# Moving mask making and small loads to GpSimd, and one more load ahead of the opening barrier, in a one-token decode block

## The chip, the cores and the metric

The kernel runs on one core of one Trainium2 chip. The metric is the device time of one execution in microseconds, measured over several executions. The profile is one of those executions, taken by the hardware profiler; its span is about 1.9 us shorter than the measured time. Times inside a profile count from the start of the span.

## The reference

One token (a row `x` of 576 numbers) goes through two branches that a gate mixes. Branch A is attention with 32 query heads over 16 key-value heads and the last 4096 positions of a cache, head size 128. Branch B is a dense layer with gelu, 576 to 4608 to 576.

```python
g = sigmoid((x * gate_w).sum(-1, keepdims=True))
# A: sliding-window attention on a cache
q = (x @ wq).reshape(B, Sq, 32, 128)
scores = einsum("bhqd,bhkd->bhqk", q, k[-4096:]) * 128**-0.5
a = einsum("bhqk,bhkd->bhqd", softmax(scores), v[-4096:]).reshape(...) @ wo
# B: dense gelu
b = gelu(x @ w1 + b1) @ w2 + b2
out = g * a + (1 - g) * b
```

All of `k`, `v`, `wq`, `wo`, `w1`, `w2` have to be read once: 53.6 MB in bf16. With one token there is little arithmetic for each byte.

## The kernel before

The large loads all go out on SyncE's queue, in the order w1, wq, k (eight halves of groups), w2 first half, v (four groups), wo, w2 second half. They share a few large buffers, tagged A to D, so a load can only be issued when the earlier tenant of its buffer has been used. The first part of w1 is moved ahead of the program's opening barrier by editing the instruction list.

```python
    def first_load_ahead(nc):
        main, body = nc.main_func.blocks[0], nc.main_func.blocks[1]
        first = next(i for i in body.instructions
                     if i.engine == mybir.EngineType.SP and type(i).__name__ == "InstDMACopy")
        body.instructions.remove(first)
        at = next(n for n, i in enumerate(main.instructions) if i.engine == mybir.EngineType.SP)
        main.instructions.insert(at, first)
    nc.at_finalize(first_load_ahead)
    # small loads, on ScalarE's queue
    nc.scalar.dma_start(out=x_row, in_=A_x.rearrange("a b d -> (a b) d"))
    nc.scalar.dma_start(out=gw_row, ...); nc.scalar.dma_start(out=b2_row, ...)
    nc.scalar.dma_start(out=b1_t, ...)
    # ... w1 (two parts) into tag "B", wq into tag "A", on nc.sync ...
```

VectorE makes the masks from an identity matrix, by reductions and sixteen small copies, and prepares `x2`, the column form of `x` that the first stage multiplies with w1 and wq:

```python
    par = ...; nc.vector.reduce_sum(out=par[:], in_=ident_f[:].rearrange("p (a t) -> p t a", t=2), axis=AX.X)
    for t in range(2):
        nc.vector.tensor_copy(out=alt[:, t : NI + 1 : 2], in_=par[:, t : t + 1].to_broadcast(...))
    # ... x doubled and turned by nine matmuls into xs_ps ...
    for t in range(2):
        nc.vector.tensor_tensor(out=x2[:, :, t], in0=xs_ps[:], in1=alt[:, t : t + NI], op=ALU.mult)
    # ... lo32, hi4, lo8, pen, pen2 by reductions ...
    for j in range(4):
        for b in range(4):
            nc.vector.tensor_copy(out=perm[:, j, b, :], in_=idv[:, j // 2, :, j % 2])
    # ... first stage: h_ps (162 matmuls on w1), gelu on VectorE, q_ps (144 matmuls on wq) ...
    for g in range(NG):
        k_t = big.tile([P, 2, SL, Dh], BF16, name="k_t", tag="CDBA"[g])   # waits for the buffer
        # ... per half: load, VectorE transposes (kt), 16 matmuls into s_ps
    nc.vector.reduce_max(out=m2[:], in_=s_ps[:].rearrange("p (n b) -> p b n", b=2), axis=AX.X)
    # ... softmax; w2 first half in tag "B"; v groups in tags "CDAC"; wo; w2 second half
```

## Time and profile before

The kernel before took 133.99 us. The table has what matters, each from the view named.

| Reading | Value | View |
|---|---|---|
| bytes moved, mean rate | 53.78 MB, 407 GB/s | page, DMA queues |
| rate while the queue is full | about 427 GB/s, DMA share about 1.0 | busy time by stretches |
| VectorE busy, GpSimd busy | 55.4 us, 0.7 us | page, engines |
| first stage (h_ps) | 12.80 to 23.02 us | timeline |
| last weights used from | 128.25 us | timeline |

First the page of the kernel before: the busy line, then busy time in forty slices of 3.3 us for the DMA engines, then the DMA queues and the chain of work that ended last.

```profile
PE 77.4 (59%) x1126; PEld 51.1 (39%) x1126; DVE 55.4 (42%) x80; ACT 12.9 (10%) x25; POOL 0.7 (1%) x6
DMA  7999998999999999999999999999999999999960
...
q8 instruction: 9, 0.15, 0.4%
q10 hardware_dynamic: 10, 0.01, 0.0%
q14 instruction: 1, 0.01, 0.0%
...
DMA 67%; PE 12%; DVE 8%; ACT 7%; issue 2%; SPq 1%; DVEq 0%
```

No engine is busy more than 59% of the span, but the DMA row reads 9 (90% or more), once 8, from the second slice nearly to the end. That points to a kernel bound by its bytes. The queue lines are packets, MB and share; the small q14 line will matter later.

Next the busy time of the engines by stretches, kernel before. The columns are the stretch, its length, busy time and count of PE, PEld, DVE, ACT and POOL, the granted clock, the DMA share and GB/s. The share can pass 1 slightly because packets are counted with the time they were under way.

```profile
4.00:20.00 16.00, 10.74 (x149) 9.60 (x150) 5.77 (x38) 0.17 (x1) 0.00 (x0) 1.00 1.04 446
20.00:60.00 40.00, 29.03 (x281) 15.74 (x281) 27.52 (x20) 1.45 (x6) 0.00 (x0) 1.00 0.99 420
60.00:100.00 40.00, 21.30 (x343) 13.52 (x341) 19.10 (x17) 9.66 (x16) 0.00 (x0) 0.75 1.00 429
100.00:126.00 26.00, 13.79 (x321) 10.76 (x322) 0.48 (x2) 0.00 (x0) 0.00 (x0) 0.59 1.00 420
```

The DMA share is 0.99 or more in all four stretches, whatever the engines do. Last, the front in the timeline of the kernel before (start, length, engine, line, operation, and in brackets the idle time before it with what ended it):

```profile
0.79 0.51 ACTq L83 DMA_DIRECT2D rows<-in_A_x_dram  x1
1.48 1.83 DVE L216 MEMSET qz_flat<- 128x2128 f32 x1 [0.39 <-issue]
6.29 0.85 DVE L117 COPY rows<-rows 1x576 bf16<-1x576 bf16 x2 [2.98 <-DMA rows<-in_A_x_dram]
11.61 0.23 DVE L130 TENSOR_TENSOR x<-xs_ps,alt 128x9 bf16<-128x9 f32 x2
23.06 0.20 DVE L228 COPY hacc<-h_ps 128x36 f32<-128x36 f32 x1 [9.39 <-PE h_ps L219]
```

The token's own 1,152 bytes were issued at 0.79 us and used at 6.29 us. w1's packets were then already under way, which is the likely reason. `x2` came at 11.6 us, behind other small VectorE work.

### The profile page before, as it was taken

What the parts mean: (1) busy time and instruction counts of PE and PEld (TensorE: products, weight loads), DVE (VectorE), ACT (ScalarE), POOL (GpSimd) and SP (SyncE); (2) the same over time, 40 slices, a digit from 0 to 9 for tenths busy, and PEclk for the clock granted to TensorE, in tenths of its full rate; (3) what the DMA queues carried; (4) which work ended last, traced back from release to release, by engine and by line L of the source; (5) the groups of instructions that cost most, each with busy time, mean ns of one, the idle gap of its engine ahead of it and who ended that gap; (6) DMA issues with size and microseconds to landing.
All of it is one profiled execution on the core that took longest, in us unless ns stands there. A gap on an engine that the chain in (4) does not pass through costs nothing.

```text
span 132.1 us, 2458 instructions
## 1 busy us (share of the span) xinstructions
PE 77.4 (59%) x1126; PEld 51.1 (39%) x1126; DVE 55.4 (42%) x80; ACT 12.9 (10%) x25; POOL 0.7 (1%) x6
## 2 busy tenths in 40 slices
PE   0038999084699769769779460007942952456651
PEld 0035999084234323223223230007942952333430
DVE  6059100503978988988985710653000000100001
ACT  3000000003000000000000059940000000000001
POOL 2000000000000000000000000000000000000000
PEclk9999999999999999999999996555555555556998
DMA  7999998999999999999999999999999999999960
GB/s 246 421 443 411 448 518 368 398 427 427 427 417 432 422 431 419 427 436 417 454 408 442 451 446 417 407 466 427 397 451 387 431 417 428 429 407 427 406 249 0
DMA packets 3190, 53.78 MB, mean 407 GB/s; under 512 B 358, under 2 KB 362, under 8 KB 620
## 3 DMA queue, kind: packets, MB, share of 16 engines
q1 hardware_dynamic: 3170, 53.61, 95.7%
q8 instruction: 9, 0.15, 0.4%
q10 hardware_dynamic: 10, 0.01, 0.0%
q14 instruction: 1, 0.01, 0.0%
HBM read 53.62 MB, written 0.00 MB: 406 GB/s over the span
## 4 chain that ended last, share of the span: by engine, by line
DMA 67%; PE 12%; DVE 8%; ACT 7%; issue 2%; SPq 1%; DVEq 0%
DMA k_t<-in_A_k_cache_dram 26%; DMA w_t<-in_B_w_dram 21%; DMA wq_t<-in_A_wq_dram 20%; ACT p_t L351 7%; PE o_ps L402 5%; DVE kt L300 3%; PE q_ps L257 3%; DVE pt L359 2%; DVE m L321 2%; PE s_ps L309 1%; PE y_ps L193 1%; SPq L415 1%; PE t_ps L377 0%; DVE out_row L437 0%; SPq L417 0%
## 5 line engine op out<-in xcount | busy, mean ns | idle before, releaser
L300 DVE STREAM_TRANSPOSE kt<-k_t 128x2048 f32<-128x2048 f32 x16 | 36.0, 2290 | 9.7 <-DMA k_t<-in_A_k_cache_dram 9.7
L309 PE MATMUL s_ps<-kt,qz_flat 128*128 128x512 bf16 x128 | 32.3, 399 | 9.2 <-DVE kt L300 9.2
L309 PEld LDWEIGHTS <-qz_flat 128*128 128x128 bf16 x128 | 12.8, 100 | 28.3 <-issue 14.7
L402 PE MATMUL o_ps<-pt,v_t 128*128 128x8 bf16 x512 | 14.6, 168 | 8.5 <-DMA v_t<-in_A_v_cache_dram 6.5
L402 PEld LDWEIGHTS <-v_t 128*128 128x128 bf16 x512 | 14.3, 104 | 8.9 <-DMA v_t<-in_A_v_cache_dram 6.7
L351 ACT ACTIVATE p_t<-s_ps,negm 128x512 bf16<-128x512 f32 x8 | 9.7, 1412 | 44.9 <-DVE negm L342 44.9
L219 PE MATMUL h_ps<-x,w_t 128*128 128x2 bf16 x162 | 10.2, 202 | 0.0
L219 PEld LDWEIGHTS <-w_t 128*128 128x128 bf16 x162 | 10.1, 169 | 0.0
L420 DVE TENSOR_TENSOR om<-o_ps,rgh 128x128 bf16<-128x128 f32 x1 | 0.3, 292 | 22.2 <-PE o_ps L402 22.2
L193 PE MATMUL y_ps<-wo_t,ov 128*1 128x288 bf16 x64 | 6.1, 364 | 4.6 <-DMA wo_t<-in_A_wo_dram 4.6
L359 DVE STREAM_TRANSPOSE pt<-p_t 128x2048 bf16<-128x2048 bf16 x2 | 4.6, 2312 | 7.4 <-ACT p_t L351 7.4
L377 PE MATMUL t_ps<-ls,ones 128*128 128x32 f32 x2 | 0.6, 396 | 11.9 <-DVE ls L375 11.9
L193 PE MATMUL y_ps<-w_t,gt 128*1 128x288 bf16 x72 | 5.6, 285 | 2.1 <-DMA w_t<-in_B_w_dram 2.1
L437 DVE CAST out_row<-y_ps 1x288 bf16<-1x288 f32 x1 | 0.4, 446 | 15.1 <-PE y_ps L193 15.1
L257 PE MATMUL q_ps<-x,wq_t 128*128 128x2 bf16 x144 | 4.0, 166 | 4.0 <-DMA wq_t<-in_A_wq_dram 4.0
L193 PEld LDWEIGHTS <-ov 128*1 128x1 bf16 x64 | 3.4, 103 | 7.0 <-issue 4.5
L257 PEld LDWEIGHTS <-wq_t 128*128 128x128 bf16 x144 | 3.9, 104 | 4.0 <-DMA wq_t<-in_A_wq_dram 4.0
L377 PEld LDWEIGHTS t_ps<-ls,ones 128*128 128x128 f32 x2 | 0.5, 310 | 12.2 <-issue 12.2
L120 PE MATMUL xs_ps<-one_b,rows 1*128 1x1 bf16 x9 | 0.7, 195 | 7.2 <-DVE rows L117 7.2
L193 PEld LDWEIGHTS <-gt 128*1 128x1 bf16 x72 | 3.2, 83 | 3.9 <-issue 2.9
L436 ACT CAST out_row<-y_ps 1x288 bf16<-1x288 f32 x1 | 0.4, 390 | 42.2 <-PE y_ps L193 42.2
L228 DVE COPY hacc<-h_ps 128x36 f32<-128x36 f32 x1 | 0.2, 196 | 9.4 <-PE h_ps L219 9.4
(68 smaller groups left out, 28.7 us busy)
## 6 DMA issues: line engine op xcount, KB each, us to landing
k_t<-in_A_k_cache_dram SPq DMA_DIRECT2D x8, 2048.0 KB, 32.3
v_t<-in_A_v_cache_dram SPq DMA_DIRECT2D x3, 4096.0 KB, 29.8
wq_t<-in_A_wq_dram SPq DMA_DIRECT2D x1, 4608.0 KB, 25.8
wo_t<-in_A_wo_dram SPq DMA_DIRECT2D x2, 2304.0 KB, 20.2
v_t<-in_A_v_cache_dram SPq DMA_DIRECT2D x2, 2048.0 KB
w_t<-in_B_w_dram SPq DMA_DIRECT2D x1, 2880.0 KB, 14.1
w_t<-in_B_w_dram SPq DMA_DIRECT2D x1, 2592.0 KB, 11.3
w_t<-in_B_w_dram SPq DMA_DIRECT2D x1, 2304.0 KB, 8.0
```

The lines of the kernel that those rows point to most:

```text
L120: nc.tensor.matmul(xs_ps[:, i : i + 1], lhsT=xdup[:, i : 2 * D : NI], rhs=one_b[0:1, 0:1], start=(i == 0), stop=(i == NI - 1), skip_group_ ...
L193: nc.tensor.matmul(y_out[s], lhsT=vec, rhs=row[:, s * DH : (s + 1) * DH], start=start, stop=stop, skip_group_check=True,)
L219: nc.tensor.matmul(h_ps[:, j:NF:NJ], lhsT=w1_t[:, i, j:FH:NJ], rhs=x2[:, i, :], start=False, stop=(i == NI - 1 and j == NJ - 1), skip_grou ...
L257: nc.tensor.matmul(q_ps[:, j : Hq : Hq // 2], lhsT=wq_t[:, i, j * Dh : (j + 1) * Dh], rhs=x2[:, i, :], start=(i == 0 and j == 0), stop=(i ...
L300: nc.vector.transpose(out=kt[:, u * half : (u + 1) * half].bitcast(FP32), in_=k_t[:, f, u * SL // 2 : (u + 1) * SL // 2, :] .rearrange("p ...
L309: nc.tensor.matmul(s_ps[:, u * 512 : (u + 1) * 512].rearrange("p (c k) -> p c k", k=32), lhsT=qz[:, h0 // 2, j, :], rhs=kv[:, u * SL // 4 ...
L321: nc.vector.reduce_max(out=m2[:], in_=s_ps[:].rearrange("p (n b) -> p b n", b=2), axis=AX.X)
L351: nc.scalar.activation(out=p_t[:, cs, :, b], in_=s_ps[:].rearrange("p (c k u b) -> p u b c k", k=8, u=2, b=2)[:, f, b % 2], func=ACT.Exp, ...
L359: nc.vector.transpose(out=pt[:, cs, :].rearrange("p c h -> p (c h)"), in_=p_t[:, cs, :, :].rearrange("p c k b -> p (c k b)"),)
L377: nc.tensor.matmul(t_ps[:], lhsT=ones[:], rhs=ls[:], start=True, stop=True)
L402: nc.tensor.matmul(o_ps[:, 8 * g : 8 * g + 8, 0], lhsT=v_t[:, c, :], rhs=pt[:, c, 8 * g : 8 * g + 8], start=(c == 0), stop=(c == NCK - 1),)
L415: nc.sync.dma_start(out=wo_t[:, r0:r1, :], in_=wo_src[:, r0:r1, :])
```

## The change

Its intent is to get the first stage going earlier: take the mask work off VectorE, make the masks with GpSimd's iota, compare and select, clear `qz_flat` there, move three small loads to GpSimd's queue, and issue x's load ahead of the opening barrier as w1's already is. The diff, cut to its core:

```diff
-    def first_load_ahead(nc):
+    def first_loads_ahead(nc):
+        for engine in (mybir.EngineType.SP, mybir.EngineType.Activation):
+            # ... the same move, for the first load of each of the two engines
-    nc.scalar.dma_start(out=gw_row, ...)   # and b2_row, b1_t
+    nc.gpsimd.dma_start(out=gw_row, ...)   # and b2_row, b1_t
-    nc.vector.memset(one_b[:], 1.0)
+    nc.gpsimd.memset(one_b[:], 1.0)
+    for base, pattern, keep in (...five masks...):
+        nc.gpsimd.iota(low[:, c0 : c0 + n], pattern=pattern, base=base, channel_multiplier=1)
+        nc.gpsimd.memset(mask[:, c0 : c0 + n], keep)
+    nc.vector.tensor_tensor(out=low[:], in0=low[:], in1=mask[:], op=ALU.bitwise_and)
+    nc.gpsimd.tensor_scalar(out=is0[:], in0=low[:], scalar1=0.0, scalar2=None, op0=ALU.is_equal)
+    nc.gpsimd.memset(perm[:], 0.0)
+    nc.gpsimd.affine_select(out=perm[:], in_=perm[:], pattern=[[-64, 2], [-1, 2], [0, 4], [-2, 32]], ...)
-    # par, alt, lo32, hi4, lo8, pen, pen2 by reductions; sixteen perm copies (all on VectorE)
-    for t in range(2):
-        nc.vector.tensor_tensor(out=x2[:, :, t], in0=xs_ps[:], in1=alt[:, t : t + NI], op=ALU.mult)
+    nc.vector.tensor_tensor(out=x2[:], in0=xs_ps[:].to_broadcast([P, NI, 2]), in1=alt, op=ALU.mult)
-    nc.vector.memset(qz_flat[:].bitcast(FP32), 0.0)
+    nc.gpsimd.memset(qz_flat[:].bitcast(FP32), 0.0)
-    # p1 = hacc * r_t, then gt = p1 * omg
+    # gt = hacc * omg * r_t in one scalar_tensor_tensor
```

More of the change, by code (lines that the diff above doesn't have):

```diff
@@ L10 @@
 BF16 = mybir.dt.bfloat16
+I32 = mybir.dt.int32
 ACT = mybir.ActivationFunctionType
@@ L51 @@
     SCALE = 1.0 / (Dh**0.5)
-    def first_load_ahead(nc):
+    def first_loads_ahead(nc):
         main, body = nc.main_func.blocks[0], nc.main_func.blocks[1]
-        first = next(
-            i
-            for i in body.instructions
-            if i.engine == mybir.EngineType.SP and type(i).__name__ == "InstDMACopy"
-        )
-        body.instructions.remove(first)
-        at = next(
-            n for n, i in enumerate(main.instructions) if i.engine == mybir.EngineType.SP
-        )
-        main.instructions.insert(at, first)
-    nc.at_finalize(first_load_ahead)
+        for engine in (mybir.EngineType.SP, mybir.EngineType.Activation):
+            first = next(
+                i
+                for i in body.instructions
+                if i.engine == engine and type(i).__name__ == "InstDMACopy"
+            )
+            body.instructions.remove(first)
+            at = next(n for n, i in enumerate(main.instructions) if i.engine == engine)
+            main.instructions.insert(at, first)
+    nc.at_finalize(first_loads_ahead)
     const = ctx.enter_context(tc.tile_pool(name="const", bufs=1))
@@ L83 @@
     nc.scalar.dma_start(out=x_row, in_=A_x.rearrange("a b d -> (a b) d"))
-    nc.scalar.dma_start(out=gw_row, in_=gate_w.rearrange("(o n) -> o n", o=1))
-    nc.scalar.dma_start(out=b2_row, in_=B_b2.rearrange("(o n) -> o n", o=1))
-    nc.scalar.dma_start(out=b1_t, in_=B_b1.rearrange("(h n) -> h n", h=2))
+    nc.gpsimd.dma_start(out=gw_row, in_=gate_w.rearrange("(o n) -> o n", o=1))
+    nc.gpsimd.dma_start(out=b2_row, in_=B_b2.rearrange("(o n) -> o n", o=1))
+    nc.gpsimd.dma_start(out=b1_t, in_=B_b1.rearrange("(h n) -> h n", h=2))
     w1_t = big.tile([P, NI, FH], BF16, name="w1_t", tag="B")
@@ L99 @@
     one_b = const.tile([1, 2], BF16, name="one_b")
-    nc.vector.memset(one_b[:], 1.0)
+    nc.gpsimd.memset(one_b[:], 1.0)
+    NCC = 2 * NI + 32 + 4 + 6
+    low = const.tile([P, NCC], I32, name="low")
+    mask = const.tile([P, NCC], I32, name="mask")
+    c0 = 0
+    for base, pattern, keep in (
+        (0, [[1, NI], [1, 2]], 1),
+        (128, [[-1, 32]], 31),
+        (128, [[-32, 4]], 96),
+        (8, [[-2, HB]], 6),
+        (4, [[-2, 2]], 2),
+    ):
+        n = 1
+        for step, num in pattern:
+            n *= num
+        nc.gpsimd.iota(low[:, c0 : c0 + n], pattern=pattern, base=base, channel_multiplier=1)
+        nc.gpsimd.memset(mask[:, c0 : c0 + n], keep)
+        c0 += n
@@ L101 @@
+    nc.vector.tensor_tensor(out=low[:], in0=low[:], in1=mask[:], op=ALU.bitwise_and)
+    is0 = const.tile([P, NCC], FP32, name="is0")
+    nc.gpsimd.tensor_scalar(
+        out=is0[:], in0=low[:], scalar1=0.0, scalar2=None, op0=ALU.is_equal
+    )
+    alt = is0[:, 0 : 2 * NI].rearrange("p (i t) -> p i t", t=2)
+    lo32 = is0[:, 2 * NI : 2 * NI + 32]
+    hi4 = is0[:, 2 * NI + 32 : 2 * NI + 36]
     ones = const.tile([P, P], FP32, name="ones")
-    nc.vector.memset(ones[:], 1.0)
+    nc.gpsimd.memset(ones[:], 1.0)
@@ L103 @@
     ident = const.tile([P, P], BF16, name="ident")
     make_identity(nc, ident[:])
-    ident_f = const.tile([P, P], FP32, name="ident_f")
-    nc.vector.tensor_copy(out=ident_f[:], in_=ident[:])
-    par = const.tile([P, 2], FP32, name="par")
-    nc.vector.reduce_sum(out=par[:], in_=ident_f[:].rearrange("p (a t) -> p t a", t=2), axis=AX.X)
-    alt = const.tile([P, NI + 1], FP32, name="alt")
-    for t in range(2):
-        nc.vector.tensor_copy(
-            out=alt[:, t : NI + 1 : 2], in_=par[:, t : t + 1].to_broadcast([P, (NI + 1) // 2])
-        )
@@ L116 @@
-    for t in range(2):
-        nc.vector.tensor_copy(out=xdup.rearrange("p (d t) -> p d t", t=2)[:, :, t], in_=x_row)
-    xs_ps = ps_m.tile([P, NI], FP32, name="xs_ps", tag="m")
+    perm = const.tile([P, 4, 4, 32], BF16, name="perm")
+    nc.gpsimd.memset(perm[:], 0.0)
+    nc.gpsimd.affine_select(
+        out=perm[:],
+        in_=perm[:],
+        pattern=[[-64, 2], [-1, 2], [0, 4], [-2, 32]],
+        compare_op=ALU.not_equal,
+        fill=1.0,
+        base=0,
+        channel_multiplier=1,
+    )
@@ new lines @@
+    ident_f = const.tile([P, P], FP32, name="ident_f")
+    nc.gpsimd.tensor_copy(out=ident_f[:], in_=ident[:])
+    lo32b = const.tile([P, 32], BF16, name="lo32b")
+    nc.gpsimd.tensor_copy(out=lo32b[:], in_=lo32)
+    pens = const.tile([P, HB + 2], FP32, name="pens")
+    nc.gpsimd.tensor_scalar(
+        out=pens[:],
+        in0=is0[:, 2 * NI + 36 : NCC],
+        scalar1=1e30,
+        scalar2=-1e30,
+        op0=ALU.mult,
+        op1=ALU.add,
+    )
+    pen = pens[:, 0:HB]
+    pen2 = pens[:, HB : HB + 2]
@@ L119 @@
+    nc.vector.tensor_copy(
+        out=xdup.rearrange("p (d t) -> p d t", t=2),
+        in_=x_row.rearrange("p (d o) -> p d o", o=1).to_broadcast([1, D, 2]),
+    )
+    xs_ps = ps_m.tile([P, NI, 1], FP32, name="xs_ps", tag="m")
     for i in range(NI):
         nc.tensor.matmul(
-            xs_ps[:, i : i + 1],
+            xs_ps[:, i, :],
             lhsT=xdup[:, i : 2 * D : NI],
@@ L128 @@
     x2 = const.tile([P, NI, 2], BF16, name="x2")
-    for t in range(2):
-        nc.vector.tensor_tensor(
-            out=x2[:, :, t], in0=xs_ps[:], in1=alt[:, t : t + NI], op=ALU.mult
-        )
-    lo32 = const.tile([P, 32], FP32, name="lo32")
-    nc.vector.reduce_sum(out=lo32[:], in_=ident_f[:].rearrange("p (a t) -> p t a", t=32), axis=AX.X)
-    lo32b = const.tile([P, 32], BF16, name="lo32b")
-    nc.vector.tensor_copy(out=lo32b[:], in_=lo32[:])
-    hi4 = const.tile([P, 4], FP32, name="hi4")
-    nc.vector.reduce_sum(out=hi4[:], in_=ident_f[:].rearrange("p (a t) -> p a t", t=32), axis=AX.X)
-    lo8 = const.tile([P, 8], FP32, name="lo8")
-    nc.vector.reduce_sum(out=lo8[:], in_=ident_f[:].rearrange("p (a c) -> p c a", c=8), axis=AX.X)
-    pen = const.tile([P, HB], FP32, name="pen")
-    nc.vector.reduce_sum(out=pen[:], in_=lo8[:].rearrange("p (b t) -> p b t", t=2), axis=AX.X)
-    nc.vector.tensor_scalar(
-        out=pen[:], in0=pen[:], scalar1=1e30, scalar2=-1e30, op0=ALU.mult, op1=ALU.add
-    )
-    pen2 = const.tile([P, 2], FP32, name="pen2")
-    nc.vector.reduce_max(out=pen2[:], in_=pen[:].rearrange("p (a b) -> p b a", b=2), axis=AX.X)
-    perm = const.tile([P, 4, 4, 32], BF16, name="perm")
-    idv = ident[:].rearrange("p (b l t) -> p b l t", b=2, t=2)
-    for j in range(4):
-        for b in range(4):
-            nc.vector.tensor_copy(out=perm[:, j, b, :], in_=idv[:, j // 2, :, j % 2])
+    nc.vector.tensor_tensor(
+        out=x2[:], in0=xs_ps[:].to_broadcast([P, NI, 2]), in1=alt, op=ALU.mult
+    )
     s0 = const.tile([1, 1], FP32, name="s0")
@@ L183 @@
     nc.vector.tensor_scalar(
-        out=gh[:, 0, :], in0=hi4[:], scalar1=g_t[:, 0:1], scalar2=None, op0=ALU.mult
+        out=gh[:, 0, :], in0=hi4, scalar1=g_t[:, 0:1], scalar2=None, op0=ALU.mult
     )
@@ L247 @@
     nc.vector.reciprocal(out=r_t[:], in_=e_h[:])
-    p1 = const.tile([P, NF], FP32, name="p1")
-    nc.vector.tensor_tensor(out=p1[:], in0=hacc[:], in1=r_t[:], op=ALU.mult)
     gt = const.tile([P, NF], BF16, name="gt")
-    nc.vector.tensor_scalar(out=gt[:], in0=p1[:], scalar1=omg[:, 0:1], scalar2=None, op0=ALU.mult)
+    nc.vector.scalar_tensor_tensor(
+        out=gt[:], in0=hacc[:], scalar=omg[:, 0:1], in1=r_t[:], op0=ALU.mult, op1=ALU.mult
+    )
     q_ps = ps_m.tile([P, Hq], FP32, name="q_ps", tag="m")
@@ L321 @@
     nc.vector.reduce_max(out=m2[:], in_=s_ps[:].rearrange("p (n b) -> p b n", b=2), axis=AX.X)
-    nc.vector.tensor_tensor(out=m2[:], in0=m2[:], in1=pen2[:], op=ALU.add)
+    nc.vector.tensor_tensor(out=m2[:], in0=m2[:], in1=pen2, op=ALU.add)
     m1 = const.tile([P, 1], FP32, name="m1")
@@ L342 @@
     nc.vector.tensor_tensor(
-        out=negm[:], in0=pen[:], in1=mb_ps[:].to_broadcast([P, HB]), op=ALU.add
+        out=negm[:], in0=pen, in1=mb_ps[:].to_broadcast([P, HB]), op=ALU.add
     )
@@ L374 @@
     ls = const.tile([P, Hq], FP32, name="ls")
-    nc.vector.tensor_scalar(out=ls[:], in0=lo32[:], scalar1=sm[:, 0:1], scalar2=None, op0=ALU.mult)
+    nc.vector.tensor_scalar(out=ls[:], in0=lo32, scalar1=sm[:, 0:1], scalar2=None, op0=ALU.mult)
     t_ps = ps_m.tile([P, Hq], FP32, name="t_ps", tag="m")
```

## The prediction

> What bounds it now: the DMA engines. Busy time by two-microsecond stretches shows near 427 GB/s and a DMA share near 1.0 from 2 to 126 us; the page counts 53.8 MB, and at 0.427 MB per us that is 126 us of a 132.1 us span. The rest is 1.2 us before bytes move and 4 us after the last weights land at 128.2 us (16 matmuls, cast, store). The chain of waits agrees: DMA 67%; its k, v and wo pieces stand there because the queue is full. The Trainium skill, "DMA: Bandwidth & Descriptors", Specifications, gives a fabric ceiling of 435 GB/s; this trace's 427 is 98% of it.
>
> What the change does. It moves no large load: SP issues w1's first part ahead of the barrier, then w1, wq, k, w2, v, wo, w2 as before. Off VectorE it takes the qz_flat clear (1.83 us), ones (0.17), sixteen perm copies (about 1.7), six mask reductions and casts (about 2 us) and, by merging, an x copy, an x2 multiply and a gelu multiply. GpSimd gets some 25 small operations (its memset took 0.2 us, its select 0.29) and three loads; I estimate 6 to 9 us for it. x's load, issued at 0.79 us and seen by VectorE at 6.3 us, will be issued near 0 and seen at 2 to 4 us. The same page, "SWDGE vs HWDGE vs iDMA", says GpSimd's queue makes descriptors in software and is slower to set up; three such issues now stand in front of one_b, which the first matmuls need.
>
> How much is on the critical path: next to nothing. The first stage's matmuls (h_ps from w1, 10.2 us, 12.8 to 23.05) may start at 9 to 11.5 us and end at 19.5 to 22. That frees w1's buffer, so k group 2 is issued 1 to 3.5 us earlier, but at 23.05 us 18.4 MB had been issued and about 9.3 moved: 21 us of data stood queued. q waits for wq's landing at 26.9 us, which is DMA order. The one tight place is v group 3, issued at 95.25 us when o_ps group 0 frees its buffer: about 42 MB issued, 40 moved, some 4.5 us queued. It hangs on the softmax after the last k, which the change doesn't touch. The end is unchanged. Waits of k's issues on semaphores shared with small loads go too (SP waited 4.0 us for x); the queue had data then.
>
> Predicted time: 133.9 us against 133.99, range 133.3 to 134.6. Chances: faster by over 2% 0.01, within 2% 0.98, slower by over 2% 0.01.
>
> What would show it: VectorE busy falls from 55.4 to about 49 us, GpSimd's rises from 0.7 to 5 to 10; the first copy of x starts at 2 to 4 us instead of 6.29; h_ps ends before 22.5; wq still lands at 26.5 to 27.3, the last k transposes start near 66.6, the last w2 piece lands near 128.2; the DMA share stays near 1.0.
>
> What would make it wrong: GpSimd's chain taking over 14 us, so that h_ps ends after wq lands; a slower DMA rate because GpSimd's descriptors share the engines; a fixed cost of a third queue at the program's start or end; uneven engines at the tail (the share falls to 0.5 from 127 to 128 us, so a few kilobytes on one engine shift the last landing by tenths of a us); the throttle, which halved the granted clock from 80 to 121 us, starting before 71 us and delaying the softmax by over 4.5 us.

## The result and the profile after

The changed kernel took 134.21 us (134.10 to 134.44, six runs) against 133.98 us (133.91 to 134.08, six runs). The ratio is 1.002, with a 95% interval of 1.0007 to 1.0033. Here and below a ratio is the mean time of one kernel's fast runs over that of the other's of the same rounds, so it is not quite the ratio of the medians quoted. VectorE does 5 us less work, and the kernel is 0.2 us slower.

The page of the changed kernel, with the lines that answer to those of before:

```profile
PE 78.4 (59%) x1126; PEld 51.4 (39%) x1126; DVE 50.3 (38%) x48; ACT 13.0 (10%) x25; POOL 7.6 (6%) x28
DMA  7999999999999999999999999999999999999950
...
q8 instruction: 9, 0.15, 0.4%
q0 software_dynamic: 96, 0.01, 0.1%
q10 hardware_dynamic: 2, 0.00, 0.0%
...
DMA 66%; PE 12%; DVE 8%; ACT 7%; issue 3%; SPq 1%; DVEq 0%
```

VectorE lost 5 us and GpSimd gained 7, as intended; the DMA row hardly moved. The q14 line is gone. The stretches of the changed kernel:

```profile
4.00:20.00 16.00, 10.54 (x148) 9.41 (x147) 2.18 (x9) 0.17 (x1) 5.04 (x14) 1.00 1.05 446
20.00:60.00 40.00, 29.10 (x275) 15.43 (x275) 27.31 (x19) 1.45 (x6) 0.00 (x0) 1.00 0.99 419
60.00:100.00 40.00, 21.90 (x343) 13.61 (x341) 19.13 (x17) 9.68 (x16) 0.00 (x0) 0.72 1.01 430
100.00:126.00 26.00, 13.81 (x321) 10.79 (x322) 0.48 (x2) 0.00 (x0) 0.00 (x0) 0.58 1.00 420
```

In the first stretch VectorE fell from 5.77 to 2.18 us, and the rates in all four stretches are the same within 1 GB/s. The front in the timeline of the changed kernel:

```profile
0.13 0.50 ACTq L83 DMA_DIRECT2D rows<-in_A_x_dram  x1
1.39 0.75 DVE L158 COPY rows<-rows 1x1152 bf16<-1x1152 bf16 x1 [1.39 <-DMA rows<-in_A_x_dram]
1.57 0.74 POOL L84 DMA_DIRECT2D rows<-in_gate_w_dram  x1 [1.13 <-POOLq L475]
3.30 0.09 POOL L100 MEMSET one_b<- 1x2 bf16 x1
7.44 0.74 DVE L179 CUSTOM_DVE_ANT_0 rows<-rows 1x576 bf16<-1x576 bf16 x1 [5.30 <-DMA rows<-in_gate_w_dram]
8.43 0.38 POOL L120 TENSOR_SCALAR is<-low 128x60 f32<-128x60 int32 x1 [3.44 <-DVE low L118]
8.84 0.18 DVE L173 TENSOR_TENSOR x<-xs_ps,is 128x18 bf16<-128x18 f32 x1 [0.52 <-POOL is L120]
22.71 0.20 DVE L250 COPY hacc<-h_ps 128x36 f32<-128x36 f32 x1 [12.38 <-PE h_ps L241]
```

x is used at 1.39 us instead of 6.29, a gain of 4.9 us. At `x2` 2.8 us of it are left (8.84 instead of 11.61): the mask step on VectorE (L118) is queued behind the gate's product, which waits for the gate weights until 7.44 us, and GpSimd idles 3.44 us for it. At the end of h_ps 0.35 us are left (22.71 instead of 23.06). Two things stand between: the b1 matmuls wait for b1's load until 10.09 us, and the product with b2 now cuts into the w1 matmuls (15.87 to 16.92 us). So even the gain in the first stage was mostly lost on the way. The question is whether it would have counted, and where the 0.2 us come from.

They lie after the last bytes. The last 16 matmuls start at 128.30 us instead of 128.25, but the span ends at 132.3 instead of 132.1. The program ends with two barriers; each engine signs off with a DRAIN and is released by an EVENT_SEMAPHORE. These are VectorE's in the kernel before, in the view of one source line (count, then shortest, median and longest in ns, then first and last start):

```profile
L464 DVEq DRAIN  x2: 19/252/484, 129.4 to 131.7; - x2
L464 DVEq EVENT_SEMAPHORE  x2: 21/21/21, 131.6 to 132.1; - x2
```

and in the changed kernel:

```profile
L486 DVEq DRAIN  x2: 128/302/477, 129.5 to 132.0; - x2
L486 DVEq EVENT_SEMAPHORE  x2: 21/21/21, 131.4 to 132.3; - x2
```

In the changed kernel VectorE is released from the first barrier 0.2 us earlier (131.4 instead of 131.6; in the trace SyncE's wait for the output store now stands last in a row of waits, where before four more of about 60 ns each followed it), but signs off for the second 0.54 us after that (131.43 to 131.97 in the trace) instead of 0.11 us. All other engines wait for it. The profile shows nothing that a DRAIN at that point would wait for: VectorE's last work ended two microseconds before.

### The profile page after: what moved, and what is told of

Its sections match the earlier page's. It is cut to its first block, busy times and chain, and to the rows that moved or that the text cites. A ratio compares the mean times of both kernels' runs of the same rounds, so it can differ in the third digit from the quotient of the medians.

```text
span 132.3 us, 2454 instructions
## 1 busy us (share of the span) xinstructions
PE 78.4 (59%) x1126; PEld 51.4 (39%) x1126; DVE 50.3 (38%) x48; ACT 13.0 (10%) x25; POOL 7.6 (6%) x28
## 4 chain that ended last, share of the span: by engine, by line
DMA 66%; PE 12%; DVE 8%; ACT 7%; issue 3%; SPq 1%; DVEq 0%
DMA k_t<-in_A_k_cache_dram 26%; DMA w_t<-in_B_w_dram 20%; DMA wq_t<-in_A_wq_dram 19%; ACT p_t L373 7%; PE o_ps L424 5%; DVE kt L322 3%; PE q_ps L279 3%; DVE pt L381 2%; DVE m L343 2%; PE s_ps L331 1%; PE y_ps L215 1%; SPq L437 1%; PE t_ps L399 0%; DVE out_row L459 0%; SPq L439 0%
## 5 line engine op out<-in xcount | busy, mean ns | idle before, releaser
L331 PE MATMUL s_ps<-kt,qz_flat 128*128 128x512 bf16 x128 | 32.8, 404 | 8.6 <-DVE kt L322 8.6
L331 PEld LDWEIGHTS <-qz_flat 128*128 128x128 bf16 x128 | 12.8, 100 | 28.2 <-issue 15.9
L190 PE MATMUL g_ps<-s,ones 1*128 1x1 f32 x2 | 0.6, 342 | 4.3 <-DVE low L118 4.3
## 6 DMA issues: line engine op xcount, KB each, us to landing
w_t<-in_B_w_dram SPq DMA_DIRECT2D x1, 2592.0 KB, 11.3
```

Source lines behind the costliest of these rows:

```text
L190: nc.tensor.matmul(g_ps[:, 0:1], lhsT=ones[0:1, 0:P], rhs=s0[0:1, 0:1], start=True, stop=True)
L331: nc.tensor.matmul(s_ps[:, u * 512 : (u + 1) * 512].rearrange("p (c k) -> p c k", k=32), lhsT=qz[:, h0 // 2, j, :], rhs=kv[:, u * SL // 4 ...
```

## The experiments

Theory A: the time is set by the bytes. The front of the program is off the critical path as long as the DMA queue holds data, and the 0.23 us come from VectorE's late last drain. The drain is late, so the theory goes, because VectorE's program, now shorter by about 30 instructions (96 to 65 in the trace, all kinds counted), enters a new block of instructions just there: the late drain is its 64th instruction. The Trainium skill, "Runtime: NRT & Kernel Launch", Instruction fetch mechanics, says that a sequencer fetches its instructions by its own DMA in blocks and that the cost of crossing into a block is mostly hidden. In the trace of before an 8,192-byte packet of the instruction queue q14 runs at 50.7 us, 1.5 us after VectorE starts its 64th instruction. In that of the changed kernel it runs at 132.6 us, after the span, and so is missing from its page. Two things in the traces speak for caution. This packet comes 0.65 us after the late drain starts, so it isn't a fetch that the drain waited for, and q14 shows no other 8,192-byte packet within the span. And with nine added clears (below) the packet runs at 35.8 us, when VectorE has started only 54 instructions.

Theory B: GpSimd's queue has a fixed cost. Theory C: issuing x's load ahead of the barrier delays the barrier (released near 1.0 us instead of 0.7) and everything after it. Theory F: the front is on the critical path, and the gain there was eaten by another cost.

### The parts of the change, alone

Masks alone (the loads as before):

```diff
-    nc.gpsimd.dma_start(out=gw_row, ...)   # and b2_row, b1_t, in the changed kernel
+    nc.scalar.dma_start(out=gw_row, ...)
-    nc.at_finalize(first_loads_ahead)
+    nc.at_finalize(first_load_ahead)
```

> The masks on GpSimd alone; x, gate, b2, b1 stay on ScalarE's queue behind the barrier. Theory A (the DMA engines set the time; the 0.23 us that the changed kernel lost lie at the program's two ends, mostly in VectorE's last drain, which came 0.54 us after its release instead of 0.11 because its now shorter program crosses into a new block of instructions just there): VectorE's program is as short as in the changed kernel, so the late drain should be here too, 134.1 to 134.35, with the last weights landing at 128.2 to 128.4. Theory B (using GpSimd's queue has a fixed cost): 133.9 to 134.05. Theory C (x's load ahead of the barrier delays the barrier and with it everything): 133.9 to 134.05.

It took 134.37 us (134.26 to 134.55, six runs). The kernel before had 134.10 us in these rounds, with nine runs from 133.76 to 134.22 and two at 135.0 and 135.3. The two are why the ratio, 1.001 with 0.997 to 1.005, shows nothing; but all six runs lie above all nine of the others. The loss is here in full, without GpSimd's queue and without the early x; by the medians it is even larger than the changed kernel's, which is taken up below. Its last drain, in the view of the source line:

```profile
L487 DVEq DRAIN  x2: 129/304/479, 129.4 to 132.1; - x2
L487 DVEq EVENT_SEMAPHORE  x2: 21/21/21, 131.6 to 132.4; - x2
```

Here the release comes at 131.6 as in the kernel before, the drain at 132.1, the end at 132.4. The time came 0.02 us above the expected range.

The loads alone (the kernel before with the three small loads on GpSimd):

```diff
-    nc.scalar.dma_start(out=gw_row, ...)   # and b2_row, b1_t
+    nc.gpsimd.dma_start(out=gw_row, ...)
```

> Only the three small loads moved to GpSimd's queue. Theory A: VectorE's program keeps its 70 rows, so no late drain, 133.9 to 134.1. Theory B: 134.15 to 134.3, the whole loss. Theory C: 133.9 to 134.05.

It took 134.00 us (133.80 to 134.09, five runs). Theory B falls: the third queue costs nothing that can be seen. Its last drain came 0.11 us after its release.

The early x alone (the kernel before with `first_loads_ahead`):

```diff
-    nc.at_finalize(first_load_ahead)
+    nc.at_finalize(first_loads_ahead)
```

> Only x's load moved ahead of the barrier. The barrier should be released about 0.26 us later (1.0 instead of 0.73 us) and x be seen near 1.4 us. Theory A: the first bytes of w1 move at 1.0 us as before, so 133.9 to 134.1. Theory C: 134.15 to 134.3. Theory B: 133.9 to 134.05.

It took 134.05 us (133.99 to 134.19, five runs). Theory C's 134.15 to 134.3 does not hold, since the median is at the level of before; a cost of up to 0.1 us can't be excluded from five runs. w1's first bytes move at 1.0 us with or without it. This run also tests the front from the side of the gain: its h_ps ran from 10.60 to 20.82 us, so it ended 2.2 us earlier than before, far more than the 0.35 us of the whole change, and nothing of that shows in the time.

### The late drain

The changed kernel, with VectorE's program brought back to its old length by copies that do nothing:

```diff
+    pad = const.tile([1, 32], BF16, name="pad")
+    for i in range(31):
+        nc.vector.tensor_copy(out=pad[:, i : i + 1], in_=gt[0:1, i : i + 1])
```

> The changed kernel with 31 one-element copies on VectorE after the gelu, in its idle time before the first k lands. They do nothing but give VectorE's program its old length. Theory A: VectorE's last drain comes 0.1 us after its release again and the program ends about 0.25 us earlier than the changed kernel: 133.85 to 134.05, though VectorE does more. Theories B and C: 134.15 to 134.3, as the changed kernel.

It took 133.99 us (133.89 to 134.06, five runs), so every run was below the changed kernel's fastest of 134.10. The changed kernel itself was not run in these rounds, but the masks alone, with the same short VectorE program, were, and took 134.26 or more. Adding 31 instructions made the kernel about 0.2 us faster. Its page and its last drain:

```profile
PE 78.6 (59%) x1126; PEld 51.4 (39%) x1126; DVE 52.3 (40%) x79; ACT 13.0 (10%) x25; POOL 7.6 (6%) x28
...
q14 instruction: 1, 0.01, 0.0%
```

```profile
L489 DVEq DRAIN  x2: 19/252/484, 129.6 to 131.7; - x2
L489 DVEq EVENT_SEMAPHORE  x2: 21/21/21, 131.6 to 132.1; - x2
```

The drain is 0.1 us after the release again, and the q14 packet is back inside the span.

The other direction: two more operations taken off VectorE, so that its program ends before the 64th instruction.

```diff
-    nc.vector.tensor_scalar(out=b2g[:], ...)        # and gh
+    nc.gpsimd.tensor_scalar(out=b2g[:], ...)
```

> The changed kernel with two more operations (the gate's b2 product and the head gates) moved from VectorE to GpSimd, so that VectorE's program ends two instructions earlier. Theory A (the late drain is the crossing into a new block of instructions, near VectorE's 64th): the crossing is no longer reached before the last drain, the drain comes 0.1 us after its release, 133.8 to 134.05, although this goes the opposite way from the padded kernel. If instead a short VectorE program as such costs time at the end: 134.15 to 134.4.

The drain came 0.1 us after its release, as theory A said:

```profile
L486 DVEq DRAIN  x2: 19/249/479, 130.6 to 132.7; - x2
L486 DVEq EVENT_SEMAPHORE  x2: 21/21/21, 132.5 to 133.1; - x2
```

The time did not settle: 134.25 us median, six runs from 133.99 to 135.21. Two of them, 134.89 and 135.21, had a mean granted clock (the share of TensorE's full clock that it was given) of 0.816 and 0.815. The profiled one is the slowest: its last 16 matmuls took 2.08 us instead of 1.15, because the clock was halved again from 128.3 us. The kernel before had two such runs, 135.0 and 135.3 (mean clock 0.816); that their clock fell at the same place isn't shown, as no trace of them was kept. The other four runs lie between 133.99 and 134.26, too wide to set them apart from either kernel; over all six the ratio to the kernel before is 1.0034, with 1.0009 to 1.0060. So it is confirmed that the drain is prompt again where it is no longer the 64th instruction, and a gain in time from trimming is not shown.

The changed kernel once more, on the same chip:

> The changed kernel itself, on the same chip as the trimmed one. Theory A: late drain again, 134.1 to 134.4, 0.15 to 0.35 us above the trimmed kernel. If its first result was the chip or chance: equal to the trimmed kernel and to the kernel before within 0.1 us.

It took 134.11 us (134.10 to 134.43) against 133.91 us of the kernel before, ratio 1.0019 with 1.0006 to 1.0032. The loss repeats, and the drain was late again. Its median is not above but below that of the trimmed kernel (134.25, with the two slow runs), so that part of the expectation missed.

How much of the loss the drain explains can be read from the profiles, as the time from VectorE's last cast to the end of the span. It is 2.71 us in the kernel before and 2.72 with the early x alone; 2.55 with the loads alone, 2.55 padded and 2.56 trimmed; 2.83 and 2.85 in the two profiles of the changed kernel; and 3.07 with the masks alone. So the late drain costs about 0.3 us (2.84 against 2.55, and 3.07 against 2.71), and the loads on GpSimd's queue give 0.16 us back through SyncE's shorter row of waits. The net of 0.12 to 0.14 us is more than half of the 0.20 to 0.23 us that the changed kernel lost; where the rest lies isn't located.

### How much room the front has

The kernel before, with clears of a `lag` tile on VectorE that the mask for `x2` has to wait for; three, nine and fourteen of them:

```diff
-    alt = const.tile([P, NI + 1], FP32, name="alt")
+    lag = const.tile([P, 2128], FP32, name="lag")
+    for _ in range(3):          # 9, 14
+        nc.vector.memset(lag[:], 0.0)
+    alt = lag[:, 0 : NI + 1]
```

> The kernel before with three added clears of 128x2128 on VectorE in front of the mask: h_ps should start at 16 to 18.5 us instead of 12.8. In the kernel before, h_ps ended 3.9 us before wq landed and the gelu 6.5 us before the first k landed, so a delay of this size should be absorbed: h_ps ends at 26 to 29, the load of w2 still goes out at 61.3 to 61.8 us, no hole in the DMA share, time within 0.3 us of the kernel before. If every microsecond of front delay counted as in the two longer delays (8 us for 17, 18 us for 28), 1.9 us or more slower.

The first stage started at 16.94 us instead of 12.80, 4.1 us late, and VectorE did 5 us more. The time was 133.88 us against 133.91, ratio 1.000 with 0.9988 to 1.0013. A delay of 4.1 us cost nothing, so theory F falls: if 4 us of delay are free, the 0.35 us that the change gained at the end of h_ps can't have counted either. The issue of w2, from the timeline of this kernel (it stands at 61.30 in that of before):

```profile
61.26 0.33 SPq L370 DMA_DIRECT2D w_t<-in_B_w_dram  x1
```

> The kernel before with nine more clears of 128x2128 on VectorE ahead of the mask that the first stage's x needs, about 16.5 us of added VectorE work, so that h_ps starts about 10 us later (near 22 us). Theory A (front off the critical path while the DMA queue holds data): h_ps ends at 31 to 33.5 us, the first k transpose starts up to 3 us late, VectorE catches up, since a pair of transposes takes 4.5 us and a k half lands each 4.9; last pair starts within 1 us of 66.6; time within 0.4 us of the kernel before. Rival F (the first stage is on the critical path and the change's gain there was eaten by another cost): 3 us or more slower.

This run and the longer one below were made before the short delay. It missed in two ways. Each clear cost 2.4 us rather than 1.83, since small operations and waits came between, so h_ps started at 30.1 us, not near 22, and it was a delay of 17.3 us. The time was 141.89 us, 7.9 more. By that number alone rival F would have won (3 us or more); but it was not the delay that was meant, and the short delay was then run to decide. The stretches of this kernel show where the time went, and they look as expected for the longer delay:

```profile
62.00:64.00 2.00, 1.70 (x9) 0.67 (x7) 2.00 (x2) 0.00 (x0) 0.00 (x0) 1.00 0.96 410
64.00:66.00 2.00, 1.70 (x8) 0.67 (x7) 2.00 (x2) 0.00 (x0) 0.00 (x0) 1.00 0.16 66
66.00:68.00 2.00, 1.71 (x8) 0.67 (x7) 2.00 (x2) 0.00 (x0) 0.00 (x0) 1.00 0.00 0
68.00:70.00 2.00, 1.70 (x9) 0.69 (x8) 2.00 (x2) 0.00 (x0) 0.00 (x0) 1.00 0.00 0
70.00:72.00 2.00, 1.70 (x9) 0.70 (x8) 2.00 (x2) 0.00 (x0) 0.00 (x0) 1.00 0.00 0
72.00:74.00 2.00, 1.70 (x9) 0.69 (x8) 2.00 (x2) 0.00 (x0) 0.00 (x0) 1.00 0.96 259
```

The DMA share falls to nothing from about 64.3 to 72.2 us. All loads up to the last k had been issued and had landed, and the next one, w2, waits for VectorE to have transposed group 2 of k. It went out at 71.28 us, 9.98 us later than in the kernel before. The hole is 7.9 us long. The profiled run is the slowest of the four, which lost between 7.1 and 9.2 us, so by the times 1 to 3 us of the 9.98 were absorbed. Counted from the packets in the trace, the stream of bytes stood 8.4 us behind the kernel before after the hole, so w2's load had about 1.5 us of room.

> The same with fourteen clears, h_ps near 31 us. Theory A: h_ps ends near 41, k transposes start near 43.5 instead of 31.9 and run back to back; the loads of w2 and v, issued when group 2 of k is transposed, go out near 70.7 instead of 61.3 us, and by then the queue, filled up to about 64 us, has been dry: 5 to 7 us slower, 139 to 141, with a hole in the DMA share of about 6 us near 65 to 71 us. If the DMA queue were not the bound, the loss would be the whole delay of 19 us or a constant share of it that the mid delay shows too.

The same mis-sizing: h_ps at 41.0 us, 28.2 us late, and 152.3 us, 18.3 more. There were two holes in the DMA share: from about 45 us, because group 2 of k waits for w1's buffer and went out at 51.2, and from about 74 to 81 us for w2, issued at 80.4. After the first hole the stream of bytes stood 8.5 us behind, so of the 28.2 us by which group 2 of k went out late, 19.7 were absorbed; the prediction had counted 21 us of queued data there. The loss is not proportional to the delay (0, 7.9 and 18.3 us for 4.1, 17.3 and 28.2 us); each run pays for the time in which the queue is empty.

### How much room the softmax has

```diff
+    for _ in range(5):
         nc.vector.reduce_max(out=m2[:], in_=s_ps[:].rearrange("p (n b) -> p b n", b=2), axis=AX.X)
```

> The kernel before with the first maximum over the scores made five times, 9.2 us more in front of the softmax. Theory A with the slack of about 4.5 us that the prediction gave for v group 3: its load goes out near 104.4 us, the queue is dry from about 100, 3 to 5 us slower: 137 to 139. If the softmax is fully on the critical path: 9.2 us slower. If there is more slack: under 2 us.

The load of v group 3 was out at 104.90 us instead of 95.25, 9.65 us later, and the time was 140.38 us, 6.4 more (6.0 in the two faster of four runs). The DMA share was 0.76, 0.04, 0.04 and 0.54 in the four stretches from 98 to 106 us, a hole of about 5.2 us. So by the times 3.2 to 3.7 us were absorbed, less than the 4.5 estimated, and the loss lies above the expected 3 to 5. Part of the profiled run's loss isn't the queue's: its clock was halved at 134.4 us and its last 16 matmuls took 2.08 us instead of 1.15. Counted from the packets, the stream of bytes stood 5.6 to 5.7 us behind after the hole, so 4.0 us were absorbed.

### Fewer bytes

A wrong result: the last 8 of 18 columns of w2's second half are left out.

```diff
-    for j0, j1 in ((0, 10), (10, 16), (16, 18)):
+    for j0, j1 in ((0, 10),):
-    for f in range(NJ, NF):
-        y_add(gt[:, f : f + 1], w2_t[:, f, :], stop=(f == NF - 1))
+    for f in range(NJ, NJ + 10):
+        y_add(gt[:, f : f + 1], w2_t[:, f, :], stop=(f == NJ + 9))
```

> A wrong result on purpose: the last 8 of 18 columns of w2's second half are neither loaded nor used, 1.18 MB less of 53.6. Theory A: 1.18 MB at 0.427 MB per us is 2.76 us less; the 20 matmuls after the last landing take 0.25 us more than the 16 did: 131.3 to 131.8. If the time were set by the engines' chain, which keeps all its steps up to the last 16 matmuls, 0 to 1.2 us less.

It took 131.91 us against 133.97, 2.06 us less, a little above the expected range. The DMA engines came to rest 2.8 us earlier, as the bytes say (about 125.7 instead of 128.5 us). But the kernel before overlaps its last small piece of w2 with the matmuls of the piece before it, and this one has 20 matmuls left after its last landing. Their first starts at 126.15 us, and the cast after them at 127.57 instead of 129.43. Leaving out 2% of the bytes saves 1.5% of the time. Taking 9% off VectorE saved nothing.

### What beats both kernels

None clearly does. The padded kernel (133.99), the loads alone (134.00) and the kernel before (133.98) are equal within what the rounds resolve.

## Why the prediction was right

The range (133.3 to 134.6) held the measured 134.21, and the class, within 2%, was right. That no gain was to be had rested on the right mechanism. The point itself, 133.9, had the wrong sign against 133.99: the 0.2 us lost at the end come from something that the prediction didn't foresee, and that they fell inside the range is the range's width and not insight.

- **Bound by the DMA engines: right.** Taking bytes away moved the end of the transfers by the predicted 2.8 us; taking 5 us from VectorE moved nothing, nor did adding 5 us to it (short delay).
- **Front off the critical path: right.** A delay of 4.1 us was free, and a gain of 2.2 us (the early x alone) brought nothing.
- **VectorE to about 49 us and GpSimd to 5 to 10: right**, 50.3 and 7.6 us.
- **h_ps before 22.5 us, with a gain of 1 to 3.5 us: missed.** It ended at 22.67 us with a gain of 0.35. The start, 11.3 us, was in the range, but the b2 product now interrupts the stage. This harmed nothing. The early x alone, with the masks still on VectorE, ended at 20.82 us, so the rest of the change gave most of the front's gain back. x came even earlier than predicted (1.39 us, not 2 to 4).
- **wq, the last k and the last w2 at the same times: right**, 27.1, 66.60 and 128.3 us.
- **"The one tight place is v group 3", with 4.5 us queued: somewhat high, and not the only one.** Its slack is 3.2 to 3.7 us by the times and 4.0 by the packets. And w2's issue at 61.3 us, which the prediction did not look at, has less, about 1.5 us by the packets. The prediction counted the queue at two issues and did not walk through all of SyncE's. It did no harm, because the change delays neither.
- **"The end is unchanged": wrong by 0.2 us.** The matmuls and the store kept their times, but VectorE's last drain came 0.54 instead of 0.11 us after its release. A VectorE program of another length (padded or trimmed) makes it prompt again, and in all three profiles with the late drain it is VectorE's 64th instruction. Why the 64th is late stays open. The fetch of a block of instructions is argued and not shown: the packets don't name their engine, the q14 packet follows the late drain instead of preceding it, and with nine added clears it comes at VectorE's 54th instruction.
- **"A fixed cost of a third queue": not seen** (134.00 us with the loads alone; the end of its profile is even 0.16 us shorter).

## What to carry to other kernels

When the DMA share is near 1 from the start to the end, as here, ask of work moved between engines whether it makes some load go out late: walk through every issue of the load queue and count how many microseconds of data stand before it, since the smallest of these numbers bounds the room that the engines have. The room here was about 2 us less than the count. Issued minus landed bytes at 0.427 MB per us (an estimate from the trace of before) give 21.8 us for group 2 of k, 3.3 for w2 and 6.1 for v group 3, where the delays found 19.7, 1.5 and 4.0. Of the difference, 1.0 to 1.3 us passed between the issue of such a load and its first packet, once the queue had run dry (71.28 to 72.25 us for w2 in the middle delay, 103.72 to 105.04 for v group 3). Follow an early gain from use to use before counting it; here 4.9 us at the load had become 0.35 us four steps later. And when a change that should be neutral moves the time by a few tenths, compare the last two microseconds of the two programs, because even the length of an instruction stream can show there.

## What the Trainium skill lacked or had wrong

- "Runtime: NRT & Kernel Launch", Instruction fetch mechanics: it gives refills in 16 KiB blocks and calls a crossing mostly hidden. Queue q8 here indeed moves nine packets of 16,384 bytes, but q14 moves blocks of 8,192. The page gives no cost for the last instructions of a program: here a last drain that was VectorE's 64th instruction came 0.43 us later than others, and cost the end about 0.3 us. That this is a crossing isn't shown.
- "DMA: Bandwidth & Descriptors": its section Anatomy of one DMA gives a fixed cost near 2 us for a DMA on GpSimd's path, and SWDGE vs HWDGE vs iDMA calls the hardware path faster to set up. Under a full queue neither decided: 1.1 KB was used 5.5 us after its issue on ScalarE's queue (0.79 to 6.29) and 5.9 us on GpSimd's (1.57 to 7.44), but 1.3 us when issued on ScalarE's ahead of the large load's packets (0.13 to 1.39).
- "GPSIMD Engine Reference", Engine selection, calls GpSimd roughly line-rate for one-input work. The two casts that moved took longer there, 0.28 instead of 0.21 us (128x128) and 0.43 instead of 0.16 us (128x32), though the profile's spans on GpSimd are rough. The clear of 128x2128 f32, which has no input, took 1.87 us on GpSimd and 1.83 us on VectorE.
